# Local attention and a tanh-shrink feed-forward on one core: FP32 loads of the second tile's q and k, two fused distance operations, slope matrices made by two engines

## The chip, the cores and the metric

The program runs on one NeuronCore of a Trainium2 chip. A core has five engines, each with its own in-order instruction stream: TensorE (PE, matmuls and transposes), VectorE (DVE), ScalarE (ACT), GpSimd (POOL) and SyncE (SP). Sixteen DMA engines move data between HBM and the on-chip memory (SBUF). A transfer is issued by SP, ACT or POOL. In the profile, the transfers that SP issues lie on queue q1, those of ACT on q10 and those of POOL on q0 ("software_dynamic"). Only the transfers on POOL's queue convert FP32 to BF16 on the way in this kernel.

The metric is the device time of one execution in microseconds (us). It is given as the median of several executions. The profile is of one further execution.

## The reference

The inputs q, k and v have the shape batch 4, heads 8, sequence 768, head size 64. The weights are 512 x 2048 and 2048 x 512. All are FP32.

```python
rel = pos[:, None] - pos[None, :]
is_global = pos[None, :] < 8
is_local = (rel >= 0) & (rel < 96)
keep = is_global | is_local
dist = where(is_global & ~is_local, 96, abs(rel))
slopes = 2.0 ** (-8.0 * (arange(8) + 1) / 8)
scores = where(keep, q @ k.T / 8 - slopes * dist, -1e9)
a = softmax(scores)
x = (a @ v)  as [3072, 512]            # tokens by heads*head size
h = x @ w_in                           # [3072, 2048]
out = (h - tanh(h)) @ w_out            # [3072, 512]
```

A query thus sees at most 96 keys before it (itself among them) and the first 8 keys of its sequence. For a tile of 128 queries this takes two tiles of keys, its own and the one before.

## The kernel before

**Tiles and steps.** The 3072 tokens are 24 tiles of 128 tokens, six for each batch. For each tile `u` the kernel loads k, q and v, transposes k and q (`T1`, `T`; `a_T`, on PE for the first eight tiles, lines 234 and 238; by DMA afterwards, line 242), and copies the transposes from PSUM to SBUF (`Te`, line 253). It then computes scores against the tile's own keys and those of the tile before (`S`, line 271), exponentiates them on ScalarE (`E`, line 279), multiplies with v (`AV`, lines 295 and 299), normalises (`R`, lines 307 and 308), and transposes the result (`X`, `Xe`, lines 322 and 331). The feed-forward follows in two matmul steps: `m1` (line 356, weights `w_in_bf`), a tanh on ScalarE and a subtraction on VectorE (lines 367 and 373), and `m2` (line 388, weights `w_out_bf`). Each weight matrix is loaded in eight pieces, named `i` (w_in) and `o` (w_out) here. One `m1` step of the first tiles needs two pieces of w_in.

**Mask and bias.** The distance term and the mask are one matrix product: `dT` holds the distances (2^20 where a key is not to be seen), `slopes` holds for each head an identity matrix times the head's negative slope. `bias` (line 128) multiplies the two. For the first three tiles this product is put into the PSUM bank before the scores are added (`B`). For the later tiles its exponential `mk` is multiplied in (lines 140 and 282). `dT` comes from an iota on GpSimd (line 100) and seven VectorE instructions (lines 106 to 118). `slopes` is eight VectorE instructions on the identity matrix `ident` (line 123), which GpSimd makes.

**Loads.** All loads but two are issued by GpSimd in one order, given by the string `LOADS` (line 408): `t` is a tile's k, q and v, `i` and `o` are weight pieces. They convert to BF16 on the way. The two exceptions are k and q of tile 0: SP and ScalarE load them as FP32 at the very start (`load_plain`, line 193), and ScalarE and VectorE convert them (`cast`, line 218).

**What sets the order.** Nothing is ordered at run time. A planner (`plan`, line 555) walks through a table of operations. Each has an engine, a planned duration, what it comes after, the buffers it takes and gives, and a priority. At each step the planner takes the operation that can start first by its own model. Operations made with `flex` may go to either of two engines. The instructions are issued to each engine in the planned order, so an engine whose next instruction waits holds up everything behind it. Gaps in PE's plan before 14 us are filled with matmuls on zeros (`warm`, line 348). Bias and scores hold one of two PSUM buffers named `big`; transposes, `m1` and `m2` share four named `one`. q and k before their transposition lie in five buffers `kq`.

Of the kernel before, what the change touches and what calls it, by code (L numbers as in the profile page):

```python
# [7 lines left out]

FP32 = mybir.dt.float32
BF16 = mybir.dt.bfloat16  # L10
AF = mybir.ActivationFunctionType
ALU = mybir.AluOpType
# [4 lines left out]
def kernel(  # L17
# [11 lines left out]
    nc = tc.nc  # L29

    B, H, S, Dh = q.shape
    P = 128
# [3 lines left out]
    G = int(n_global)  # L36
    L = int(n_local)
    scale = 1.0 / float(Dh) ** 0.5
    BIG = 2.0 ** 20

    DM = moe_w_in.shape[0]
    DFF = moe_w_in.shape[1]
# [4 lines left out]
    NV = 12  # L47
    KQ = 5
    ROWS = 4
    APART = 4  # L50
    BIASED = 3
    PE_T, PE_X = 8, 9
    HT = 3
    TJ = 4
# [9 lines left out]
        return (0, u, N0) if u < N0 else ((u - N0) // HT + 1, (u - N0) % HT, HT)  # L64

    cpool = ctx.enter_context(tc.tile_pool(name="const", bufs=1))
    stpool = ctx.enter_context(tc.tile_pool(name="stage", bufs=1))
    bpool = ctx.enter_context(tc.tile_pool(name="bpool", bufs=KQ))
    kpool = ctx.enter_context(tc.tile_pool(name="kpool", bufs=9))
    ppool = ctx.enter_context(tc.tile_pool(name="ppool", bufs=3))  # L70
# [9 lines left out]
    ident = cpool.tile([P, P], BF16, name="ident")  # L80
    mk = cpool.tile([P, H, 3, P], BF16, name="mk")
    dist = cpool.tile([P, 2, P], FP32, name="dist")
    tmp01 = cpool.tile([P, 2, 2, P], FP32, name="tmp01")
# [14 lines left out]
    def prepare():  # L98
        make_identity(nc, ident)
        nc.gpsimd.iota(  # L100
            dist, pattern=[[P, 2], [-1, P]], base=0, channel_multiplier=1,
            allow_small_or_imprecise_dtypes=True,
        )

    def dist_mask():
        nc.vector.tensor_scalar(
            out=tmp01[:, 0], in0=dist, scalar1=0.0, scalar2=BIG, op0=ALU.is_lt, op1=ALU.mult
        )
        nc.vector.tensor_scalar(
            out=tmp01[:, 1], in0=dist, scalar1=float(L), scalar2=BIG, op0=ALU.is_ge, op1=ALU.mult  # L110
        )
        nc.vector.tensor_tensor(out=tmp01[:, 0], in0=tmp01[:, 0], in1=tmp01[:, 1], op=ALU.max)
        nc.vector.tensor_tensor(out=dT[:, 1:3, :], in0=dist, in1=tmp01[:, 0], op=ALU.max)
        nc.vector.tensor_copy(out=dT[:, 0, :], in_=dT[:, 1, :])
        nc.vector.tensor_scalar(
            out=dT[:, 0, 0:G], in0=dT[:, 0, 0:G], scalar1=float(L), scalar2=None, op0=ALU.min
        )
        nc.vector.memset(dT[:, 2, 0:G], float(L))

    def build_slopes():  # L120
        for h in range(H):
            slope = 2.0 ** (-8.0 * (h + 1) / H)
            nc.vector.tensor_scalar(  # L123
                out=slopes[:, slot(h), :], in0=ident, scalar1=-slope / scale, scalar2=None, op0=ALU.mult
            )

    def bias(dst, m, a, stop):
# [20 lines left out]
    PE, ACT, DVE, POOL, SP = ENG.PE, ENG.Activation, ENG.DVE, ENG.Pool, ENG.SP  # L148
# [6 lines left out]
    def op(key, eng, us, fn, after=(), take=(), give=(), pri=0, dma=0.0, alt=None):  # L155
        ops[key] = dict(
            key=key, eng=eng, us=us, fn=fn, alt=alt, after=[a for a in after if a is not None],
            take=list(take), give=list(give), pri=pri, dma=dma,
        )

# [14 lines left out]
    kf, qf, vf = {}, {}, {}  # L175
    kq = {}
# [40 lines left out]
    def cast(u, j, src, eng):  # L217
        copy_on(eng)(out=kq_of(u)[:, j, :], in_=src.pop(u).rearrange("p a x -> p (a x)"))
# [186 lines left out]
    AHEAD = 5.0  # L405
    WARM = (1.3, 14.0)
    T_ROWS, T_LD, T_W, T_ST, T_DT, T_DX = 0.66, 0.95, 1.29, 0.7, 1.75, 0.9
    LOADS = "tttiiitiiitoooiotoiooot"
    first, n_of = [], {"t": 0, "i": 0, "o": 0}
    for c in LOADS + "t" * NU:  # L410
        if n_of[c] < (NU if c == "t" else WJ):
# [3 lines left out]
    prev = None  # L415
# [6 lines left out]
    for it in first:  # L422
        if it[0] != "t":
            load(it, 0.75, lambda it=it: load_w(it), T_W)
            continue
        u = it[1]
        for nm in ("vf", "kf", "qf") if u == 0 else ("kf", "qf", "vf"):
            key = ("ld", nm, u)
            if u == 0 and nm != "vf":
                op(key, SP, 0.6 if nm == "kf" else 0.0, lambda: None, dma=T_ROWS)  # L430
                continue
            after = []
            if nm == "vf" and u >= NV:
                after += [("AV", u - NV + 1), ("V", (u - NV) // NQ * NQ + NQ - 2)]
            rows = u < ROWS and nm != "vf"
            load(key, 0.7 if rows else 0.88, lambda u=u, nm=nm: load_bf(u, nm), T_ROWS if rows else T_LD,
                 after=after, take=["kq"] if nm == "kf" else [])
        if u == 0:
            op(("prep",), POOL, 0.7, prepare, after=[("issue", prev)])
            prev = ("prep",)  # L440

    op(("dT",), DVE, 2.0, dist_mask, after=[("prep",)], pri=-2)
    op(("sl",), DVE, 0.9, build_slopes, after=[("prep",), ("issue", ("dT",))], pri=-2)

    def flex(key, us, fn, **kw):
        alt = [(e, t) for e, t in us]
        op(key, alt[0][0], alt[0][1], fn, alt=alt, **kw)
# [3 lines left out]
    for g, us in enumerate(groups):  # L451
        b, o, n, m = shape1(g)
# [3 lines left out]

    for m in range(3):
        for a in range(2):
            op(("mk", m, a), PE, 0.22, lambda m=m, a=a: a_mk(m, a), after=[("dT",), ("sl",), ("AV", 1)],
               take=["one"], pri=1)  # L460
            op(("mke", m, a), ACT, 0.52, lambda m=m, a=a: a_mke(m, a), after=[("mk", m, a)],
               give=["one"], pri=1)

    for u in range(NU):
        i = u % NQ
        rk, rq, rv = ("ld", "kf", u), ("ld", "qf", u), ("ld", "vf", u)
        if u == 0:
            op(("cq", u), ACT, 0.45, lambda u=u: cast(u, 0, qf, ACT), after=[rq], take=["kq"], pri=-1)
            op(("ck", u), DVE, 0.55, lambda u=u: cast(u, 1, kf, DVE), after=[rk, ("issue", ("cq", u))], pri=-1)
            rk, rq = ("ck", u), ("cq", u)  # L470
        go = [key for a, key in prog if a <= u - AHEAD]
        late = [("issue", ("T", u - 1)) if u else None, go[-1] if go else None]
# [16 lines left out]
        if u < BIASED:  # L489
            for o in os:  # L490
                op(("B", u, o), PE, 0.44, lambda u=u, o=o: a_B(u, o), pri=1,
                   after=[("dT",), ("sl",), ("issue", ("B", u, 0) if o else ("S", u - 1, 0)) if u or o else None],
                   take=["big"])
# [41 lines left out]
    for u in range(NU):  # L535
        g = group_of[u]
        m = shape1(g)[3]
# [17 lines left out]
    def plan():  # L555
# [2 lines left out]
        avail = {n: [0.0] * c for n, c in bufs.items()}  # L558
        free = {PE: WARM[0], ACT: 2.8, DVE: 1.5, POOL: 0.85, SP: 0.7}
        avail["one"][0] = WARM[1]  # L560
        ring = {SP: [0.0, []], POOL: [0.0, []]}
        share = {SP: 0.35, POOL: 0.65}
        done, start = {}, {}
        f1 = f2 = 0.0
# [9 lines left out]
        while waiting or any(queues.values()):  # L574
# [46 lines left out]
            end = t + o["us"]  # L621
            free[o["eng"]] = end
            start[key] = t
            if o["dma"]:
# [39 lines left out]
        return sorted(order, key=lambda x: x[0])  # L664

    with tc.manual_schedule(engines={PE, ACT, DVE, POOL, SP}):
        load_plain(0, "kf")
        load_plain(0, "qf")
        for i in range(2):
            nc.vector.memset(vb[i][:, :, Dh : Dh + 1], 1.0)  # L670
        nc.vector.memset(zero, 0.0)
        for i in range(2, NV):
            nc.vector.memset(vb[i][:, :, Dh : Dh + 1], 1.0)
        for t, key in with_warm(order):
            ops[key]["fn"]()
# [35 lines left out]
```

## Time and profile before

| what | value |
|---|---|
| median of 6 executions | 221.61 us (218.98 to 222.41) |
| profiled execution, its time | 221.1 us |
| its span, first to last instruction | 219.3 us |
| PE busy | 207.9 us (95%) |
| DVE, ACT, POOL busy | 132.7, 124.8, 73.1 us |
| warming matmuls within PE's busy time (line 348) | 4.9 us |
| granted TensorE clock | 1.0 in every stretch asked for |
| DMA queue of POOL (q0) | 13.37 MB |
| DMA queues of SP (q1) and ACT (q10) | 12.72 and 0.26 MB |

Times within the profile count from the start of the span. "Busy" is the time in which an engine executes. Matmuls are pipelined, so PE's busy time is not PE at its peak. The bytes of a queue are counted as they are written: a converting load reads twice what it is credited with. The profile's DMA share is the mean busy share of the sixteen DMA engines; it can be over 1[...]. A "landing" is the time from the start of a transfer's issue to its completion.

### The profile page before, as it was taken

How to read it: one execution, taken by the hardware profiler on the slowest of the kernel's cores; microseconds unless marked ns; L12 is line 12 of the kernel's file. 1: busy time of each engine (PE TensorE's matmuls, PEld its weight loads, DVE VectorE, ACT ScalarE, POOL GpSimd, SP SyncE). 2: the span in 40 equal slices, each digit the busy share in tenths (PEclk: the TensorE clock that was granted, in tenths of full speed). 3: DMA queues.
4: the chain of work that ended last, by engine and by line, in shares of the span. 5: the costliest groups of instructions: out<-in, count | busy, mean ns of one | idle time of the engine just before them, and what ended most of it. 6: DMA issues, size and time to landing. Idle time of an engine off the chain costs nothing.

```text
span 219.3 us, 5048 instructions
## 1 busy us (share of the span) xinstructions
PE 207.9 (95%) x2019; PEld 127.7 (58%) x2048; DVE 132.7 (61%) x285; ACT 124.8 (57%) x206; POOL 73.1 (33%) x93
## 2 busy tenths in 40 slices
PE   7779999999999999899979999999999999999994
PEld 2545997787766555455545555555555555555553
DVE  5536887668758866467647566666874744444311
ACT  3448988666558556565654754686564455544310
POOL 7968668798354604441327040000000000000000
PEclk9999999999999999999999999999999999999999
DMA  8999999999999999999999999331342121011112
GB/s 134 135 171 187 186 186 197 170 182 149 122 176 156 181 131 184 201 157 114 140 176 117 151 67 148 99 108 40 96 113 36 45 72 49 6 46 48 48 51 96
DMA packets 103960, 26.68 MB, mean 122 GB/s; under 512 B 92416, under 2 KB 100992, under 8 KB 103936
## 3 DMA queue, kind: packets, MB, share of 16 engines
q0 software_dynamic: 74592, 13.37, 79.9%
q1 hardware_dynamic: 29072, 12.72, 29.2%
q10 hardware_dynamic: 272, 0.26, 0.5%
q8 instruction: 16, 0.26, 0.5%
q14 instruction: 8, 0.07, 0.1%
HBM read 27.26 MB, written 6.29 MB: 153 GB/s over the span
## 4 chain that ended last, share of the span: by engine, by line
PE 82%; DMA 11%; POOL 2%; DVE 2%; issue 1%; POOLq 0%
PE one L356 35%; PE one L388 34%; DMA qk<-kq 8%; PE big L271 5%; DMA kq<-in_k_dram 4%; PE big L295 2%; PE big L299 2%; POOL w_in_bf L212 1%; PE one L322 1%; PE one L234 1%; POOL vb L199 1%; PE one L238 1%; DVE slopes L123 1%; PE one L128 0%; PE big L128 0%
## 5 line engine op out<-in xcount | busy, mean ns | idle before, releaser
L356 PE MATMUL one<-xT,w_in_bf 128*128 128x128 bf16 (+1 forms) x768 | 98.8, 273 | 1.6 <-DMA w_in_bf<-in_moe_w_in_dram 1.6
L367 ACT ACTIVATE th<-one 128x384 f32<-128x384 f32 (+1 forms) x120 | 61.2, 516 | 58.2 <-PE one L356 56.7
L388 PE MATMUL one<-w_out_bf,g 128*128 128x512 bf16 (+2 forms) x390 | 92.3, 362 | 1.7 <-issue 0.6
L373 DVE TENSOR_TENSOR g<-one,th 128x384 bf16<-128x384 f32 (+1 forms) x120 | 68.5, 581 | 40.6 <-ACT th L367 39.2
L356 PEld LDWEIGHTS <-w_in_bf 128*128 128x128 bf16 x768 | 58.8, 98 | 33.8 <-DMA w_in_bf<-in_moe_w_in_dram 2.1
L388 PEld LDWEIGHTS <-g 128*128 128x128 bf16 x416 | 37.6, 98 | 32.8
L205 POOL DMA_DIRECT2D kq<-in_k_dram x20 | 17.7, 885 | 43.7 <-DMA qk<-kq 37.5
L279 ACT ACTIVATE pd<-big 128x1024 bf16<-128x1024 f32 x24 | 24.6, 1023 | 5.0 <-PE big L271 5.0
L199 POOL DMA_DIRECT2D vb<-in_v_dram x24 | 21.5, 896 | 5.5 <-DMA kq<-in_k_dram 3.5
L282 DVE TENSOR_TENSOR pd<-pd,mk 128x1024 bf16<-128x1024 bf16 x21 | 14.5, 690 | 11.4 <-ACT pd L279 11.4
L279 ACT ACTIVATE po<-big 128x1024 bf16<-128x1024 f32 x20 | 20.5, 1026 | 1.1 <-PE big L271 1.1
L398 ACT COPY ot<-one 128x512 f32<-128x512 f32 (+1 forms) x19 | 10.9, 575 | 13.3 <-PE one L388 12.3
L205 POOL DMA_DIRECT2D kq<-in_q_dram x20 | 17.8, 890 | 1.8 <-DMA vb<-in_v_dram 0.8
L308 DVE TENSOR_TENSOR x<-big,rden 128x512 bf16<-128x512 f32 x24 | 16.6, 692 | 0.8
L271 PE MATMUL big<-qk 64*128 64x128 bf16 x352 | 14.4, 218 | 2.1 <-DMA qk<-kq 2.1
L271 PEld LDWEIGHTS <-qk 64*128 64x128 bf16 x352 | 9.9, 94 | 8.9 <-issue 4.8
L282 DVE TENSOR_TENSOR po<-po,mk 128x1024 bf16<-128x1024 bf16 x18 | 12.4, 690 | 2.9 <-ACT po L279 2.9
L295 PE MATMUL big<-vb,pd 128*128 128x65 bf16 x192 | 14.0, 193 | 0.0
L295 PEld LDWEIGHTS <-pd 128*128 128x128 bf16 x192 | 12.5, 97 | 1.8
L299 PE MATMUL big<-vb,po 128*128 128x65 bf16 x160 | 12.4, 193 | 0.0
L299 PEld LDWEIGHTS <-po 128*128 128x128 bf16 x160 | 10.4, 97 | 1.3
L398 DVE COPY ot<-one 128x512 f32<-128x512 f32 (+1 forms) x7 | 4.0, 578 | 8.9 <-PE one L388 7.0
(45 smaller groups left out, 85.3 us busy)
## 6 DMA issues: line engine op xcount, KB each, us to landing
out_dram<-ot SPq DMA_DIRECT2D x23, 256.0 KB, 2.8
vb<-in_v_dram POOLq DMA_DIRECT2D x24, 128.0 KB, 7.6
kq<-in_k_dram POOLq DMA_DIRECT2D x23, 128.0 KB, 7.0
kq<-in_q_dram POOLq DMA_DIRECT2D x23, 128.0 KB, 7.6
w_in_bf<-in_moe_w_in_dram POOLq DMA_DIRECT2D x8, 256.0 KB, 8.6
w_out_bf<-in_moe_w_out_dram POOLq DMA_DIRECT2D x8, 256.0 KB, 8.7
qf<-in_q_dram ACTq DMA_DIRECT2D x1, 256.0 KB, 3.4
kf<-in_k_dram SPq DMA_DIRECT2D x1, 256.0 KB, 4.0
```

The costliest lines, as they stand in the source:

```text
L199: i = nc.gpsimd.dma_start(out=vb[u % NV][:, :, 0:Dh], in_=by_head)
L205: i = nc.gpsimd.dma_start(out=dst.rearrange("p (h d) -> p h d", d=Dh), in_=by_head)
L271: nc.tensor.matmul(s[:, slot(2 * p + hh), :], qk[u - o][r, 1, p, :], qk[u][r, 0, p, :], start=u >= BIASED, stop=True, skip_group_check=u < ...
L279: nc.scalar.activation(pr[u, o], s, AF.Exp, bias=0.0, scale=scale)
L282: nc.vector.tensor_tensor(out=pr[u, o], in0=pr[u, o], in1=mk[:, :, mask_of(u, o), :], op=ALU.mult)
L295: nc.tensor.matmul(dst, pr[u, 0][:, slot(h), :], vb[u % NV][:, h, :], start=True, stop=last,)
L299: nc.tensor.matmul(dst, pr[u, 1][:, slot(h), :], vb[(u - 1) % NV][:, h, :], start=False, stop=True,)
L308: nc.vector.tensor_tensor(out=xs[u].rearrange("q (a h) d -> q a h d", a=2), in0=t[:, :, :, 0:Dh], in1=rden.to_broadcast([P, 2, H // 2, Dh] ...
L356: nc.tensor.matmul(t[:, (f - f0) * n : (f - f0 + 1) * n], w_in_bf[j][:, c, fo : fo + P], xT[b][:, c, o : o + n], start=(c == 0), stop=(c = ...
L367: nc.scalar.activation(h_view(ths[g, f0], g), h_view(hs[g, f0], g), AF.Tanh, bias=0.0, scale=1.0)
L373: nc.vector.tensor_tensor(out=gs[b][:, f0 : f0 + m, o : o + n], in0=h_view(hs.pop((g, f0)), g), in1=h_view(ths.pop((g, f0)), g), op=ALU.su ...
L388: nc.tensor.matmul(os_[u, part][:, 0 : hi - lo], gs[b][:, f, t * P : (t + 1) * P], w_out_bf[f // FJ][:, f % FJ, lo:hi], start=(f == 0), st ...
```

## The change

- **Loads.** k and q of tile 1 are loaded like those of tile 0: FP32, k by SP and q by ScalarE, issued directly behind those of tile 0 at the start, then converted on ScalarE or VectorE as the planner chooses (`PLAIN = 2`, two staging buffers each). The two converting loads of GpSimd go away. In `LOADS`, the fourth piece of w_in moves ahead of tile 3's k, q and v.
- **Planner.** The plan takes the four FP32 loads as landed at given times, 4.1 and 4.8 us (q and k of tile 0) and 1.4 us later for tile 1. GpSimd's transfers are modelled as starting to move at 5.2 us. The conversions of both tiles go to either engine (`flex`).
- **Distances.** Of the seven VectorE instructions, the copy, the cap and the memset stay. The two comparisons and the two maxima over 128 x 256 elements become four `scalar_tensor_tensor` instructions over 128 x 128, two for each half (`distance_0`, `distance_1`). For this GpSimd makes a second iota, `over`. The bias of a tile's own keys waits for the first half only.
- **Slopes.** Each of the eight is an operation of its own; VectorE makes two and ScalarE six, by an activation with a scale.
- **Start.** VectorE fills the identity's zeros instead of GpSimd; GpSimd, instead of VectorE, sets the ones column of the first v buffer.

```diff
-    LOADS = "tttiiitiiitoooiotoiooot"
+    LOADS = "tttiiiitiitoooiotoiooot"
...
-            if u == 0 and nm != "vf":
-                op(key, SP, 0.6 if nm == "kf" else 0.0, lambda: None, dma=T_ROWS)
+            if u < PLAIN and nm != "vf":
+                op(key, SP, 0.0, lambda: None, at=(4.8 if nm == "kf" else 4.1) + 1.4 * u, pri=-3,
+                   take=["kq"] if nm == "kf" else [])
                 continue
...
+    def unit():
+        nc.gpsimd.affine_select(
+            out=ident, in_=ident, compare_op=ALU.not_equal, fill=1.0, base=0,
+            pattern=[[-1, P]], channel_multiplier=1,
+        )
+
+    def numbers():
+        for t, base in ((dist, 0), (over, 1 - L)):
+            nc.gpsimd.iota(
+                t, pattern=[[P, 2], [-1, P]], base=base, channel_multiplier=1,
+                allow_small_or_imprecise_dtypes=True,
+            )
+
+    def distance(a):
+        n = slice(a, a + 1)
+        nc.vector.scalar_tensor_tensor(
+            out=dist[:, n], in0=dist[:, n], scalar=-FAR, in1=dist[:, n], op0=ALU.mult, op1=ALU.max
+        )
+        nc.vector.scalar_tensor_tensor(
+            out=dT[:, 1 + a, :], in0=over[:, a], scalar=FAR, in1=dist[:, a], op0=ALU.mult, op1=ALU.max
+        )
...
+    def slope(h, eng):
+        f = -(2.0 ** (-8.0 * (h + 1) / H)) / scale
+        if eng is ACT:
+            nc.scalar.activation(slopes[:, slot(h), :], ident, AF.Copy, bias=0.0, scale=f)
+        else:
             nc.vector.tensor_scalar(
-                out=slopes[:, slot(h), :], in0=ident, scalar1=-slope / scale, scalar2=None, op0=ALU.mult
+                out=slopes[:, slot(h), :], in0=ident, scalar1=f, scalar2=None, op0=ALU.mult
             )
...
-    op(("dT",), DVE, 2.0, dist_mask, after=[("prep",)], pri=-2)
-    op(("sl",), DVE, 0.9, build_slopes, after=[("prep",), ("issue", ("dT",))], pri=-2)
+            op(("ident",), POOL, 0.3, unit, after=[("issue", prev)])
+            op(("nums",), POOL, 0.7, numbers, after=[("issue", ("ident",))])
+            prev = ("nums",)
+
+    op(("dT", 0), DVE, 1.0, distance_0, after=[("nums",)], pri=-2)
+    op(("dT", 1), DVE, 0.6, distance_1, after=[("nums",), ("issue", ("dT", 0))], pri=-1)
+    for h in range(H):
+        eng = DVE if h < 2 else ACT
+        op(("sl", h), eng, 0.14 if h < 2 else 0.22, lambda h=h, eng=eng: slope(h, eng), after=[("ident",)], pri=-3)
...
-        if u == 0:
-            op(("cq", u), ACT, 0.45, lambda u=u: cast(u, 0, qf, ACT), after=[rq], take=["kq"], pri=-1)
-            op(("ck", u), DVE, 0.55, lambda u=u: cast(u, 1, kf, DVE), after=[rk, ("issue", ("cq", u))], pri=-1)
+        if u < PLAIN:
+            flex(("cq", u), [(ACT, 0.55), (DVE, 0.6)], lambda eng, u=u: cast(u, 0, qf, eng), after=[rq], pri=-1)
+            flex(("ck", u), [(DVE, 0.6), (ACT, 0.55)], lambda eng, u=u: cast(u, 1, kf, eng), after=[rk], pri=-1)
...
-        ring = {SP: [0.0, []], POOL: [0.0, []]}
+        ring = {SP: [0.0, []], POOL: [5.2, []]}
...
-        load_plain(0, "kf")
-        load_plain(0, "qf")
-        for i in range(2):
-            nc.vector.memset(vb[i][:, :, Dh : Dh + 1], 1.0)
+        nc.gpsimd.memset(vb[0][:, :, Dh : Dh + 1], 1.0)
+        for u in range(PLAIN):
+            load_plain(u, "kf")
+            load_plain(u, "qf")
+        nc.vector.memset(ident, 0.0)
         nc.vector.memset(zero, 0.0)
-        for i in range(2, NV):
+        for i in range(1, NV):
             nc.vector.memset(vb[i][:, :, Dh : Dh + 1], 1.0)
```

More of the change, by code (lines that the diff above doesn't have):

```diff
@@ L6 @@
 from concourse._compat import with_exitstack
-from concourse.masks import make_identity
 FP32 = mybir.dt.float32
@@ L38 @@
     scale = 1.0 / float(Dh) ** 0.5
-    BIG = 2.0 ** 20
+    FAR = 2.0 ** 20
     DM = moe_w_in.shape[0]
@@ L51 @@
     BIASED = 3
+    PLAIN = 2
     PE_T, PE_X = 8, 9
@@ L66 @@
     cpool = ctx.enter_context(tc.tile_pool(name="const", bufs=1))
-    stpool = ctx.enter_context(tc.tile_pool(name="stage", bufs=1))
+    stpool = ctx.enter_context(tc.tile_pool(name="stage", bufs=PLAIN))
     bpool = ctx.enter_context(tc.tile_pool(name="bpool", bufs=KQ))
@@ L82 @@
     dist = cpool.tile([P, 2, P], FP32, name="dist")
-    tmp01 = cpool.tile([P, 2, 2, P], FP32, name="tmp01")
+    over = cpool.tile([P, 2, P], FP32, name="over")
     dT = cpool.tile([P, 3, P], BF16, name="dT")
@@ L95, in slot, with distance_0 @@
         return (h % 2) * NP + h // 2
[L98 to L102, printed above, removed]
-        )
-    def dist_mask():
-        nc.vector.tensor_scalar(
-            out=tmp01[:, 0], in0=dist, scalar1=0.0, scalar2=BIG, op0=ALU.is_lt, op1=ALU.mult
-        )
-        nc.vector.tensor_scalar(
-            out=tmp01[:, 1], in0=dist, scalar1=float(L), scalar2=BIG, op0=ALU.is_ge, op1=ALU.mult
-        )
-        nc.vector.tensor_tensor(out=tmp01[:, 0], in0=tmp01[:, 0], in1=tmp01[:, 1], op=ALU.max)
-        nc.vector.tensor_tensor(out=dT[:, 1:3, :], in0=dist, in1=tmp01[:, 0], op=ALU.max)
+    def unit():
+        nc.gpsimd.affine_select(
+            out=ident, in_=ident, compare_op=ALU.not_equal, fill=1.0, base=0,
+            pattern=[[-1, P]], channel_multiplier=1,
+        )
+    def numbers():
[8 more added lines that the diff above has]
+            out=dist[:, n], in0=dist[:, n], scalar=-FAR, in1=dist[:, n], op0=ALU.mult, op1=ALU.max
+        )
+        nc.vector.scalar_tensor_tensor(
+            out=dT[:, 1 + a, :], in0=over[:, a], scalar=FAR, in1=dist[:, a], op0=ALU.mult, op1=ALU.max
+        )
+    def distance_0():
+        distance(0)
         nc.vector.tensor_copy(out=dT[:, 0, :], in_=dT[:, 1, :])
@@ L117, in dist_mask, with distance_1 @@
         )
+    def distance_1():
+        distance(1)
         nc.vector.memset(dT[:, 2, 0:G], float(L))
-    def build_slopes():
-        for h in range(H):
-            slope = 2.0 ** (-8.0 * (h + 1) / H)
+    def slope(h, eng):
[3 more added lines that the diff above has]
+        else:
             nc.vector.tensor_scalar(
-                out=slopes[:, slot(h), :], in0=ident, scalar1=-slope / scale, scalar2=None, op0=ALU.mult
+                out=slopes[:, slot(h), :], in0=ident, scalar1=f, scalar2=None, op0=ALU.mult
             )
@@ L153, in copy_on, with op @@
         return {ACT: nc.scalar.copy, DVE: nc.vector.tensor_copy, POOL: nc.gpsimd.tensor_copy}[eng]
-    def op(key, eng, us, fn, after=(), take=(), give=(), pri=0, dma=0.0, alt=None):
+    def op(key, eng, us, fn, after=(), take=(), give=(), pri=0, dma=0.0, alt=None, at=None):
         ops[key] = dict(
-            key=key, eng=eng, us=us, fn=fn, alt=alt, after=[a for a in after if a is not None],
+            key=key, at=at, eng=eng, us=us, fn=fn, alt=alt, after=[a for a in after if a is not None],
             take=list(take), give=list(give), pri=pri, dma=dma,
@@ L438 @@
         if u == 0:
-            op(("prep",), POOL, 0.7, prepare, after=[("issue", prev)])
-            prev = ("prep",)
-    op(("dT",), DVE, 2.0, dist_mask, after=[("prep",)], pri=-2)
-    op(("sl",), DVE, 0.9, build_slopes, after=[("prep",), ("issue", ("dT",))], pri=-2)
+            op(("ident",), POOL, 0.3, unit, after=[("issue", prev)])
[6 more added lines that the diff above has]
+        op(("sl", h), eng, 0.14 if h < 2 else 0.22, lambda h=h, eng=eng: slope(h, eng), after=[("ident",)], pri=-3)
+    biased_by = [("dT", 0)] + [("sl", h) for h in range(H)]
     def flex(key, us, fn, **kw):
@@ L458 @@
         for a in range(2):
-            op(("mk", m, a), PE, 0.22, lambda m=m, a=a: a_mk(m, a), after=[("dT",), ("sl",), ("AV", 1)],
+            op(("mk", m, a), PE, 0.22, lambda m=m, a=a: a_mk(m, a), after=biased_by + [("dT", 1), ("AV", 1)],
                take=["one"], pri=1)
@@ L491 @@
                 op(("B", u, o), PE, 0.44, lambda u=u, o=o: a_B(u, o), pri=1,
-                   after=[("dT",), ("sl",), ("issue", ("B", u, 0) if o else ("S", u - 1, 0)) if u or o else None],
+                   after=biased_by + [("dT", 1) if o else None,
+                                    ("issue", ("B", u, 0) if o else ("S", u - 1, 0)) if u or o else None],
                    take=["big"])
@@ L623, in plan @@
             start[key] = t
-            if o["dma"]:
+            if o["at"]:
+                done[key] = o["at"]
+            elif o["dma"]:
                 via = POOL if o["eng"] is POOL else SP
```

## The prediction

> **What bounds the kernel now.** I read the page's engine rows first, then PE's busy time by stretches, then the time line and the chain of the first 20 us, then the DMA views.
>
> PE is busy 95% of the span, so the end is PE's work plus the time PE loses. The busy time by stretches, PE alone, says where it loses time (columns: stretch, its length, busy time, instructions, clock, DMA share, GB/s):
>
> ```profile
> 0.00:2.00 2.00, 0.75 (x2) 1.00 0.00 0
> 2.00:4.00 2.00, 2.00 (x6) 1.00 0.80 223
> 4.00:6.00 2.00, 1.56 (x4) 1.00 1.81 190
> 14.00:16.00 2.00, 0.65 (x9) 1.00 1.39 190
> 20.00:22.00 2.00, 2.00 (x31) 1.00 1.62 187
> 22.00:80.00 58.00, 57.26 (x814) 1.00 1.92 170
> 80.00:120.00 40.00, 37.68 (x316) 1.00 1.61 152
> ```
>
> From 22 to 80 us PE loses 0.7 us. From 0 to 22 us its busy times sum to 17.6 us, but 4.9 of these are the matmuls on zeros (line 348), so the useful work is 12.7 and the loss 9.3 us. The change touches only this start, and can win only some of the 9.3. The time line shows what they are:
>
> ```profile
> 1.24 1.00 POOL L199 DMA_DIRECT2D vb<-in_v_dram  x1 [0.80 <-DVE vb L673]
> 3.17 0.29 DVE L106 TENSOR_SCALAR tmp<-dist 128x256 f32<-128x256 f32 x1 [1.61 <-POOL dist L100]
> 4.51 0.89 POOL L199 DMA_DIRECT2D vb<-in_v_dram  x1
> 4.85 0.57 DVE L114 COPY dT<-dT 128x128 bf16<-128x128 bf16 x1
> 5.65 1.15 DVE L123 TENSOR_SCALAR slopes<-ident 128x128 bf16<-128x128 bf16 x7
> 6.48 0.59 DVE L218 CAST kq<-kf 128x512 bf16<-128x512 f32 x1
> 6.50 0.72 PE L128 MATMUL big<-slopes,dT 128*128 128x512 bf16 x2 [0.94 <-DVE slopes L123]
> 7.16 2.03 PE L238 MATMUL one<-ident,kq 128*64 128x128 bf16 x32
> 14.60 0.62 PE L356 MATMUL one<-xT,w_in_bf 128*128 128x128 bf16 x8 [0.88 <-DMA w_in_bf<-in_moe_w_in_dram]
> 15.97 0.62 PE L356 MATMUL one<-xT,w_in_bf 128*128 128x128 bf16 x8 [0.75 <-DMA w_in_bf<-in_moe_w_in_dram]
> 18.00 0.63 PE L238 MATMUL one<-ident,kq 128*64 128x128 bf16 x8 [0.27 <-DMA kq<-in_k_dram]
> ```
>
> PE's first useful work is at 6.50, behind VectorE's distances and slopes. The conversion of k0 waits behind them too: k0 landed at 4.74 (issue at 0.74, 4.0 to landing), but the conversion starts at 6.48 and PE transposes at 7.16. Later PE waits 0.88, 0.75 and 0.27 us for weights and for k of tile 3, 1.9 in sum. While it waits, the work behind waits too, since PE's order is fixed.
>
> Asked one issue at a time, the DMA view gives the landings on POOL's queue (start of issue + time to landing): v0 5.7, k1 6.3, q1 7.0, v1 9.2, k2 9.9, q2 10.6, v2 13.2, w_in pieces 14.6, 15.9, 17.2, k3 18.0, q3 18.6, v3 19.6. The seconds' stretches show how full the DMA is (the last column is GB/s as written):
>
> ```profile
> 3.00:4.00 1.00, 1.00 (x4) 0.39 (x3) 0.79 (x3) 0.00 (x0) 1.00 (x3) 1.00 1.05 362
> 6.00:7.00 1.00, 0.49 (x2) 0.10 (x1) 1.00 (x8) 0.00 (x0) 1.00 (x3) 1.00 1.18 124
> 7.00:8.00 1.00, 1.00 (x17) 0.84 (x18) 0.06 (x1) 0.17 (x1) 1.00 (x2) 1.00 1.51 109
> ```
>
> Before 2 us nothing moves; from 3 to 4 us the FP32 loads of tile 0 run alone at 362 GB/s; near 7 us the rate dips (73 GB/s in the quarter 6.50 to 6.75), because v1, issued from 4.51 to 5.40, is not yet flowing and k1 and q1 are through.
>
> **The parts, costed.** The sum is against the profiled execution, 221.1 us with a span of 219.3; the 1.8 us around the span I leave as they are. The median, 221.6, is 0.5 above it; my forecast for the median is 221.6 minus the gain.
>
> *POOL's stream.* Two issues go (line 203, 0.71 us each: -1.42). The fill of the identity goes to VectorE (-0.23), a second iota comes (+0.35). The v0 issue now waits for POOL's own small memset (four like it take 0.10 each), not for VectorE: it starts at about 0.9 instead of 1.24 (bounds 0.8 and 1.24). So v1, k2, q2, v2 and the weights are issued 1.42 + 0.23 + 0.3 - 0.35 = 1.6 us earlier.
>
> *The transfers.* k1 and q1 took 0.55 and 0.7 us between landings on POOL's queue, 1.25 together. As FP32 they write 0.52 MB; at 362 GB/s that is 1.45 us, but on the same engines. Here the Trainium skill speaks against the change: "DMA: Bandwidth & Descriptors", section "Rules for kernel authors", says that spreading loads over several issuing engines gives no bandwidth, only issue time. By that rule the weights gain nothing (+0.2 by the numbers). By the rows they gain the dip at 6.5 to 7.4 us, when the engines have little to move since POOL has not issued yet: about half of 0.9 us, and part of the second wide gap (v2's 2.6 us against 1.0 for v3, with issues far ahead). Bounds for the second piece of w_in, which `m1` needs: from +0.2 to -(1.2 + 1.6 + 0.6) = -3.4, if v1 and v2 also fall to 1.0. The nearest rows are v1's and v2's own, so I keep their durations and take -0.6 + 0.2, rounded to -0.5: 15.4 us.
>
> *When FP32 q1 and k1 land.* They queue behind tile 0's on SP and ACT. At 3.7 us some 0.32 MB of 1.05 have moved (the quarter-second rates before, added up), and v0 starts to flow. The other 0.73 MB take 1.95 us alone, and v0, then v1 cost 0.9 us each: 6.5 with v0's part alone, 7.5 with both. I take 7.0, converted at 7.6.
>
> *VectorE.* From about 2.95 (POOL's iotas) it runs four fused operations. No such row exists; the nearest are a two-input operation over 256 elements, 0.42, and a one-input one over 128, 0.16, so 0.28 each, bounds 0.16 and 0.42. With the copy (0.16 to 0.57: the 0.57 ended with POOL's v1 issue at 5.40), the cap (0.17) and the memset (0.07), all is done at 4.5 to 5.2. The conversion of k0 then starts on landing, 4.75 to 5.2, instead of 6.48.
>
> *ScalarE.* A second DMA issue (0.71) goes ahead of the table load, which ends at 3.5 instead of 2.76. Six slopes follow: lines 279 and 367 give 1.02 us for 1024 and 0.60 for 512 elements, so 0.27 for 128; bounds 0.16 and 0.37 (the copy of 256). They end at 5.1. Queued behind them is q0's conversion, 5.1 to 5.7 instead of 4.13 to 4.75; its reader on PE comes after k0's transposes, so the cost hides. The last slope releases the first bias at 5.1 instead of 6.50.
>
> *PE.* Bias at 5.1, transposes of k0 at 5.4, of q0 at 5.9, then a wait until 7.6 for tile 1 with about 0.8 us of bias and scores to fill it. Work begins 1.4 us earlier, of which 0.3 are lost waiting: 1.1 won. With the bias earlier, tile 0's exponential starts near 7.9 instead of 9.56, and PE has more attention to do before it reaches `m1`.
>
> *Order of loads.* k3 comes behind a fourth piece of w_in: one 1.3 us step later, 18.8 after the other gains. Two pieces let PE do `m1` for three tiles, 0.9 us each: 2.7 us, which covers the 0.8. Without that cover it costs 0.8.
>
> Sum: 1.1 from the start and 0.5 from the weights: **1.6 us**, 219.5 for a profiled execution, **220.0** as a median. After 22 us PE stays the bound, so the shift carries to the end.
>
> **Rivals.**
>
> *Large gain (218.6).* With a deeper backlog v1 and v2 take about 1.7 us each instead of 2.2 and 2.6; the weights come 1.4 us earlier still, which takes away the rest of PE's waits for weights (0.88 + 0.75, of which 0.5 are counted): 1.6 + 1.4 = 3.0 us, if attention fills PE until then. For it: v3 took 1.0. Against: v2 had its issue ahead and still took 2.6.
>
> *No gain (221.6).* The rule holds: the engines are full, k1 and q1 land at 7.6, which with conversion is 8.2, when PE transposed tile 1 before (the second half of the 32 from 7.16). What VectorE wins is spent on warming matmuls. Or the new order of the whole plan costs later what it wins: the stretch from 80 to 120 us loses 2.3 us to single waits for transposing DMAs, and these may move either way.
>
> *Slower (223.8).* One mechanism: PE stands at tile 1's transposes. In the old order all 32 transposes run ahead of the first scores. If FP32 and converting loads share the engines by turns from 3.7 us on, the FP32 loads get two thirds of the mixed 160 to 187 GB/s (5 to 6 us), some 115: 0.73 MB take 6.3 us and land at 10.0. Conversion and transposes then come at 10.6 instead of 8.2, 2.4 us late, less 0.2 for weights. It decides from a landing of 7.6 on and costs over 1% from about 9.8. Against: at 4.00 to 4.25 both flowed and 305 GB/s were moved. For: the plan assumes 5.5 and 6.2, so all is ordered for an early landing.
>
> That the change does nothing it says is not open: the issues are fixed in the program.
>
> **How the numbers follow.** Within 1% (2.2 us) a measurement of this kernel hardly tells a change; six runs spread over 3.4 us. The likeliest case (gain 0.8 to 2.8) has 0.46: 0.19 of it below 219.4, 0.27 within 1%. Large gain 0.19, faster. No gain 0.15, within. Slower 0.20: 0.18 beyond 1%, 0.02 within. In sum 0.38, 0.44, 0.18. The likeliest case alone spans 218.8 to 220.8. The range for 8 in 10 goes from 217.9 (the large gain and 0.7 for the runs' spread) to 223.2 (most of the slower case).
>
> **What the profile after would show.** Bias matmuls near 5.1 and transposes near 5.4; q1 and k1 landed by 7.0, no PE wait over 1 us at tile 1's transposes; POOL's v1 issue near 2.9; the second w_in piece at 15.4 or before; PE full from about 20 us. Wrong would be: a landing of k1 after 9 us, exponentials of tile 0 not before 9, or a loss after 22 us that is more than 1.5 us off the 7.0 of before (0.7 to 80 us, 2.3 to 120 us, 4.0 for the rest and the last stores).

## The result, and the profile after

The changed kernel takes 0.9944 of the time before, with a 95% interval of 0.9925 to 0.9963. On the 221.09 us before (median of 64 executions) this is a gain of 1.2 us (0.8 to 1.7). The median after is 219.73 us (29 executions). All ratios leave out executions that took over 1.5% longer than the fastest of their kernel, here five of the 29. The profiled executions differ by 1.8 us: 219.3 against 221.1, with spans of 217.5 and 219.3. The forecast was 1.6 us. The sum came out near, but two of its terms did not: the first scores came 0.3 us earlier where 1.1 were forecast, and the weights 2.5 us earlier instead of 0.5.

PE's busy time by stretches, PE alone, with the columns as in the prediction. First a row of the kernel before, then the changed kernel:

```profile
0.00:14.00 14.00, 11.37 (x102) 1.00 1.15 139
```

```profile
0.00:14.00 14.00, 10.71 (x111) 1.00 1.28 182
...
14.00:16.00 2.00, 1.95 (x35) 1.00 1.45 195
...
22.00:80.00 58.00, 57.26 (x790) 1.00 1.92 168
80.00:120.00 40.00, 37.41 (x316) 1.00 1.57 154
```

The busy times from 0 to 22 us sum to 18.2 us, of which 3.5 are matmuls on zeros. The loss is 7.3 us instead of 9.3. Without the matmuls on zeros (4.9 and 3.5 us, all before 14 us) PE has done 7.2 us of work by 14 us instead of 6.5. From 14 to 22 us it does 7.5 instead of 6.2, most of it from 14 to 16 us, where it is busy for 1.95 us instead of 0.65. From 22 to 80 us nothing changes. From 80 to 120 us PE loses 0.3 us more. This makes 1.7 of the 1.8 us of the span.

The first scores and the first exponential of the kernel before:

```profile
9.12 0.40 PE L271 MATMUL big<-qk 64*128 64x128 bf16 x8
...
9.56 1.02 ACT L279 ACTIVATE pd<-big 128x1024 bf16<-128x1024 f32 x1 [0.21 <-PE big L271]
```

The time line of the changed kernel:

```profile
3.29 0.89 POOL L212 DMA_DIRECT2D vb<-in_v_dram  x1
...
4.59 0.95 PE L141 MATMUL big<-slopes,dT 128*128 128x512 bf16 x2 [0.58 <-DVE dist L113]
...
4.98 0.43 DVE L231 CAST kq<-kf 128x512 bf16<-128x512 f32 x1
...
5.65 0.62 ACT L231 CAST kq<-qf 128x512 bf16<-128x512 f32 x1 [0.41 <-DMA qf<-in_q_dram]
...
7.51 0.69 DVE L231 CAST kq<-kf 128x512 bf16<-128x512 f32 x1 [2.11 <-DMA kf<-in_k_dram]
...
8.25 0.63 PE L251 MATMUL one<-ident,kq 128*64 128x128 bf16 x8 [1.15 <-DVE kq L231]
...
8.82 0.40 PE L284 MATMUL big<-qk 64*128 64x128 bf16 x8
...
9.26 1.02 ACT L292 ACTIVATE pd<-big 128x1024 bf16<-128x1024 f32 x1 [1.83 <-PE big L284]
...
13.81 1.07 PE L369 MATMUL one<-xT,w_in_bf 128*128 128x128 bf16 x16
```

The bias is out at 4.59 us instead of 6.50, and k0 is converted at 4.98 instead of 6.48. But k1 lands only at 7.5 us. Its transposes stand ahead of the first scores in PE's order, so PE waits 1.15 us and the scores start at 8.82. That is 0.3 us earlier than before. The last line is the other half: both `m1` steps run in one go at 13.81, with no wait for weights.

The landings on GpSimd's queue, taken from the DMA view one issue at a time:

| | v1 issued | v0 lands | v1 takes | v2 takes | second w_in piece lands |
|---|---|---|---|---|---|
| before | 4.5 | 5.7 | 2.2 | 2.6 | 15.9 |
| after | 3.3 | 7.8 | 0.9 | 0.9 | 13.4 |

"Takes" is the time since the landing ahead of it in the queue. v0 lands 2.1 us later than before, since it shares the DMA engines with the FP32 loads. v1 and v2 behind it then take less than half the time.

What the queue moved from the landing ahead of v1 to that of the second w_in piece stands in the next two rows (packets, MB, mean busy share of the sixteen engines), first for the kernel before (6.99 to 15.92 us), then for the changed one (7.75 to 13.42 us):

```profile
q0 software_dynamic: 4112, 1.35, 137.9%
```

```profile
q0 software_dynamic: 2983, 1.07, 160.4%
```

This makes 151 GB/s before and 189 after. From share, length and number follows the mean time of a packet, 48 ns before and 49 after. So the packets did not take longer before; fewer were under way at a time. The queue is practically alone here, so a share over 1 means that the times of packets of one queue overlap within an engine. The second difference is in the bytes. The transfers from v1 to the second w_in piece (four of 128 KB, two of 256 KB) hold 1.05 MB in both kernels. Before, 0.3 MB more had been moved when that piece was complete. This points to engines that were already at the transfers behind it while others still had part of it to do; the trace does not name the engine of a packet.

Stretches of 1 us (PE alone; the last column is GB/s as written) show the same. The first row is from the kernel before, the others from the changed one:

```profile
11.00:12.00 1.00, 1.00 (x17) 1.00 1.24 150
```

```profile
7.00:8.00 1.00, 0.10 (x1) 1.00 1.90 178
...
11.00:12.00 1.00, 0.93 (x18) 1.00 1.46 198
```

From 7 to 8 us the kernel before moved 109 GB/s at a share of 1.51.

### The profile page after: what moved, and what is told of

The parts are those of the page before. It is cut to its first block, busy times and chain, and to the rows that moved or that the text cites. A ratio compares the mean times of both kernels' runs of the same rounds, so it can differ in the third digit from the quotient of the medians.

```text
span 217.5 us, 5049 instructions
## 1 busy us (share of the span) xinstructions
PE 206.6 (95%) x2016; PEld 127.1 (58%) x2044; DVE 132.1 (61%) x278; ACT 127.3 (59%) x215; POOL 72.0 (33%) x92
## 4 chain that ended last, share of the span: by engine, by line
PE 81%; DMA 12%; POOL 4%; issue 1%; DVE 0%; POOLq 0%
PE one L369 35%; PE one L401 34%; DMA qk<-kq 8%; PE big L284 5%; DMA kq<-in_q_dram 4%; PE big L308 2%; PE big L312 2%; POOL w_in_bf L225 1%; POOL vb L212 1%; PE one L247 1%; POOL kq L216 1%; PE one L335 1%; PE one L141 0%; PE one L251 0%; POOL over L106 0%
## 5 line engine op out<-in xcount | busy, mean ns | idle before, releaser
L411 ACT COPY ot<-one 128x512 f32<-128x512 f32 (+1 forms) x19 | 10.9, 574 | 13.3 <-PE one L401 12.9
```

## The experiments

All ratios are against the kernel before, run on the same chip in the same session. The row of the changed kernel is the measurement above, so it is compared with the others across sessions. Every reading of a trace is of one profiled execution.

| kernel | executions counted | ratio | 95% interval |
|---|---|---|---|
| changed kernel | 24 of 29 | 0.9944 | 0.9925 to 0.9963 |
| undo_loads | 21 of 22 | 0.9962 | 0.9946 to 0.9979 |
| loads_alone | 18 of 22 | 0.9932 | 0.9909 to 0.9955 |
| undo_order | 15 of 16 | 0.9940 | 0.9919 to 0.9962 |
| pool_delay | 18 of 20 | 1.0039 | 1.0016 to 1.0063 |
| dummy_loads | 10 of 10 | 0.9970 | 0.9938 to 1.0003 |
| k1_true | 5 of 5 | 0.9892 | 0.9865 to 0.9919 |
| k1_true_again | 9 of 9 | 0.9907 | 0.9876 to 0.9938 |
| loads_alone_k1 | 10 of 10 | 0.9919 | 0.9884 to 0.9955 |
| scores_first | 6 of 6 | 0.9898 | 0.9853 to 0.9943 |
| v0_late | 3 of 6 | 0.9873 | 0.9813 to 0.9932 |
| v0_late_scores_first | 18 of 19 | 0.9915 | 0.9887 to 0.9942 |
| warm_fill | 6 of 6 | 0.9855 | 0.9802 to 0.9909 |

### Loads or vector work

`undo_loads` takes the FP32 loads of tile 1 back and keeps the rest:

```diff
-    PLAIN = 2
+    PLAIN = 1
...
-        ring = {SP: [0.0, []], POOL: [5.2, []]}
+        ring = {SP: [0.0, []], POOL: [0.0, []]}
```

> The changed kernel with k and q of tile 1 again as converting loads of GpSimd (and the plan's start of GpSimd's transfers back at 0); distances, slopes and the order of loads stay as changed. Theory 'loads': the gain comes from weights that land 2.5 us earlier because GpSimd's queue has two transfers fewer; then the second piece of w_in lands at 15 us or later, PE waits for it again (over 1 us in sum before 20 us), and the time is 220.6 to 221.3, like before. Rival 'vector work': the gain comes from bias and conversions that start 1.9 us earlier; then the time stays at 219.5 to 220.0.

The ratio is 0.9962 (220.1 us). The second w_in piece lands at 15.2, v1 and v2 take 1.9 and 2.0 us, and PE waits 0.8 us for weights (over 1 was expected) and 2.3 for k of later tiles. So the weights are back where the theory "loads" put them. The time lies between the two theories: 0.4% of gain stay (0.2 to 0.5).

`loads_alone` is the kernel before with the FP32 loads, their times in the plan, their conversions by either engine and the order of loads from the change. Distances and slopes stay as they were:

```diff
...
+            if u < PLAIN and nm != "vf":
+                op(key, SP, 0.0, lambda: None, at=(4.8 if nm == "kf" else 4.1) + 1.4 * u, pri=-3,
+                   take=["kq"] if nm == "kf" else [])
...
+        for u in range(PLAIN):
+            load_plain(u, "kf")
+            load_plain(u, "qf")
```

> The kernel before with only the loads changed: FP32 loads of tile 1, the plan's times for them and the fourth piece of w_in ahead of tile 3; distances and slopes as before, all on VectorE, identity and its zeros by GpSimd. Theory 'loads': 219.6 to 220.3, the second piece of w_in lands by 14 us, no wait of PE for weights. Rival 'vector work': 220.8 to 221.5, first scores not before 9 us.

The ratio is 0.9932. The second w_in piece lands at 13.3, v1 and v2 take 1.1 and 1.0 us, and PE does not wait for weights. The first exponential starts at 9.11, 0.15 us before that of the changed kernel, though the vector work is the old one. The loads alone therefore bring all of the gain that can be measured. The vector work, with the new order of loads, brings 0.4% alone and nothing measurable on top. The two do not add.

### Why the weights come earlier

`pool_delay` keeps the FP32 loads and puts five iotas that nobody needs behind GpSimd's own two. v1 is then issued at 5.5 instead of 3.3 us:

```diff
...
+        for _ in range(5):
+            nc.gpsimd.iota(
+                idle, pattern=[[P, 2], [-1, P]], base=0, channel_multiplier=1,
+                allow_small_or_imprecise_dtypes=True,
+            )
```

> The changed kernel with five more iotas on GpSimd (into a tile that nobody reads) behind its own two: 1.9 us, so that v1 is issued at about 5.2, as far ahead of its turn as in the kernel before; the FP32 loads stay. Theory 'lead': v1 and v2 took 2.2 and 2.6 us in the kernel before because their descriptors were written only just ahead; then v2 takes over 1.8 us between landings again, the second piece of w_in lands at 15 us or later and the time goes to 220.5 or more. Rival 'two transfers fewer': v1 and v2 keep their 0.9 us, the second piece lands by 14.2, the time within 0.6 of the changed kernel.

The ratio is 1.0039, so a delay of 2.2 us on GpSimd costs all of the gain and more. v1 takes 1.3 and v2 1.6 us (over 1.8 was expected), the two w_in pieces behind them 1.9 and 2.4 us. The second lands at 16.9, 3.5 us later than in the changed kernel, which is more than the delay itself. The first row is from this kernel, the second from the changed one:

```profile
14.00:15.00 1.00, 1.00 (x11) 1.00 1.38 159
```

```profile
14.00:15.00 1.00, 1.00 (x24) 1.00 1.44 195
```

`dummy_loads` goes the other way. It is the kernel before with two useless FP32 loads behind those of tile 0:

```diff
+        for nm, src, eng in (("kx", k, nc.sync), ("qx", q, nc.scalar)):
+            eng.dma_start(out=stpool.tile([P, 2, TJ * Dh], FP32, name=nm), in_=rows_of(src, 1))
```

> The kernel before with two useless loads added: k and q of tile 1 as FP32 by SP and ScalarE into tiles that nobody reads, behind those of tile 0; GpSimd still loads them converting, and all else is as before. 0.52 MB more are moved. Theory 'lead': the FP32 loads hold GpSimd's transfers back until about 7.5 us while their descriptors pile up; then v1 and v2 take 0.9 to 1.3 us between landings instead of 2.2 and 2.6, and the second piece of w_in lands at 14.6 to 15.9, no later than before in spite of the added bytes; time within 0.6 of before. Rival 'bytes': it lands 1.4 us later, 17.3, and the time rises by 1 us or more.

v0 lands at 8.1 us, then v1 and v2 take 1.0 us each, and the second w_in piece lands at 15.6. That is 0.3 us earlier than before, although 0.52 MB more were moved ahead of it and GpSimd issued it at the same time (8.44). The ratio is 0.9970, with an interval that just touches 1, although the first exponential starts at 10.92, 1.4 us later than before. From 14 us on the rate is that of the changed kernel:

```profile
14.00:15.00 1.00, 1.00 (x15) 1.00 1.45 197
```

Both runs agree with the lead and not with the number of bytes. The lead is here the time from the start of v1's issue to the landing ahead of it. It is 2.5 us in the kernel before, 2.6 in `undo_loads` and 2.1 in `pool_delay`, and there v1 takes 1.3 to 2.2 us. It is 3.9 to 5.4 us in the eleven others, and there v1 takes 0.9 to 1.2 us.

The lead of v1 is not the whole of it. v2 had a lead of 3.8 us in the kernel before and took 2.6 us; in `k1_true_again` it had the same and took 1.0. And a landing can be late with a long lead: in `k1_true` the fourth w_in piece was issued 5.6 us before the landing ahead of it and still landed 2.6 us behind it. Why fewer packets are under way after a short lead no run here shows.

### The order of loads

`undo_order` puts the fourth piece of w_in back behind tile 3:

```diff
-    LOADS = "tttiiiitiitoooiotoiooot"
+    LOADS = "tttiiitiiitoooiotoiooot"
```

> The changed kernel with the old order of loads (fourth piece of w_in behind tile 3's k, q, v). Theory 'loads': the first two pieces still land at 13.4, k3 at about 15.5, the fourth piece at about 19; PE has 2.7 us less feed-forward work to fill up with between 16 and 19 us but tile 3 earlier: within 0.4 us of the changed kernel, 219.5 to 220.1. Rival 'order': the swap itself is what wins, and the time goes back to 220.7 or more.

The ratio is 0.9940, as for the changed kernel. k3 lands at 15.1 and the fourth piece at 18.3. The swap is worth nothing that can be measured.

### PE's wait for k1

`k1_true` sets the plan's landing times to those of the trace:

```diff
-                op(key, SP, 0.0, lambda: None, at=(4.8 if nm == "kf" else 4.1) + 1.4 * u, pri=-3,
+                op(key, SP, 0.0, lambda: None, at={"kf": (4.8, 7.5), "qf": (4.2, 5.65)}[nm][u], pri=-3,
```

> The changed kernel with the plan's landing times of the four FP32 loads set to those of the trace (q 4.2 and 5.65, k 4.8 and 7.5 us instead of 4.1 and 5.5, 4.8 and 6.2), nothing else. The first scores then stand ahead of tile 1's transposes on PE. Theory 'late k1': they start near 7.5 instead of 8.8, the exponential near 8 instead of 9.26, and the time falls by 0.4 to 1.2 us, to 218.5 to 219.3. Rival 'transfers set it': PE is fed by the weights from 13.4 us on whatever stands ahead, and the time stays within 0.3 of 219.7.

The ratio is 0.9892 (218.76 us). The same kernel was run a second time:

> The kernel of k1_true once more (the plan's landing times set to those of the trace), for more executions: 218.5 to 219.0, ratio 0.987 to 0.992.

It gave 0.9907. The scores start ahead of tile 1's transposes, as expected, at 7.7 us in the first profile. In the second:

```profile
7.38 0.40 PE L284 MATMUL big<-qk 64*128 64x128 bf16 x8
...
8.25 1.10 PE L251 MATMUL one<-ident,kq 128*64 128x128 bf16 x16
```

But the plan's later orders changed too, so this alone does not say which step wins. The same times on top of `loads_alone` give `loads_alone_k1`:

> The kernel before with the loads changed as in loads_alone, and the plan's landing times set to those of the trace as in k1_true; distances and slopes as before, all on VectorE. Theory 'late k1 hides the vector work': with k1's wait out of the way, the later bias (6.5 instead of 4.6 us) delays the first scores to about 9 instead of 7.5, and the time is 0.4 to 1.2 above k1_true, 219.2 to 220.0. Rival 'vector work is worth nothing': within 0.3 of k1_true.

The median is 219.56 us against 219.37 for `k1_true_again` in the same session (0.9919 and 0.9907). The scores start at 8.70 there, 1.3 us later, and this costs nothing that can be measured: 0.3 us, give or take 1.0 (an estimate from the two intervals).

Two runs changed one step and left all else in the plan's order. `scores_first` issues the first scores ahead of tile 1's transposes (`ahead`, in the lines left out, moves one step of the order in front of another):

```diff
     order, model_end = plan()
...
+    ahead(("S", 0, 0), ("T1", 1))
```

> The changed kernel with its plan unchanged but for one step: the first scores (tile 0) are issued ahead of the transposes of tile 1's k. All later orders are those of the changed kernel. Theory 'late k1': PE's wait for k1 (1.2 us at 8.25) no longer holds the scores; they start at 7.5 instead of 8.8, the exponential of tile 0 at 8.0 instead of 9.26, PE's loss before 22 us falls from 7.3 to 6.3 to 6.9 us, and the time falls by 0.4 to 1.0, to 218.7 to 219.3. Rival 'tile 1 sets it': the chain through tile 1's exponentials starts at k1's landing in any case, time within 0.3 of the changed kernel.

The ratio is 0.9898, but the gain did not come in the expected way. The scores start at 9.02, not at 7.5. In this execution q1 lands at 7.4 instead of 5.65, and ScalarE's order has the conversion of q1 ahead of the copy that the scores need:

```profile
7.37 0.62 ACT L231 CAST kq<-qf 128x512 bf16<-128x512 f32 x1 [2.13 <-DMA qf<-in_q_dram]
7.90 1.06 ACT L266 COPY qk<-one 128x512 bf16<-128x512 bf16 x2
```

`v0_late` lets GpSimd make the identity and the iotas first and issue v0 behind them, at 1.9 us instead of 1.28 (2.4 was expected):

```diff
...
+    ahead(("nums",), ("ld", "vf", 0))
+    ahead(("ident",), ("nums",))
```

> The changed kernel with its plan unchanged but for one step: GpSimd makes the identity and the two iotas first and issues v of tile 0 behind them, at about 2.4 instead of 1.28 us. Theory 'sharing': the FP32 loads run alone for 0.9 us longer, so k1 lands at 6.0 to 6.4 instead of 7.5 and q1 at 5.3 to 5.6; conversion and transposes of tile 1 start at 7.0 instead of 8.25; time 218.6 to 219.3. The weights' landings stay (13.4 for the second piece, within 0.4). Rival 'the second load on SP is late by itself': k1 still lands after 7.2 and the time stays within 0.3 of the changed kernel.

k1 lands at 6.4 us, as expected from less sharing, and tile 1's transposes start at 7.13 instead of 8.25. The second w_in piece lands at 12.9 (13.0 or later was expected). The ratio is 0.9873, with a wide interval, from three executions. The other three had a mean clock of 0.991 or 0.992 and took 221.6 to 221.9 us.

`v0_late_scores_first` does both:

> Both steps: v of tile 0 issued behind the iotas, and the first scores ahead of tile 1's transposes. If both act on the same wait of PE for k1, the two gains do not add: within 0.3 us of the better of the two, 218.5 to 219.2. If the start of the exponentials counts by itself, 218.2 to 218.6.

The ratio is 0.9915. The gains do not add. The point values of all these kernels lie below the changed kernel's, by 0.2 to 0.7% of the time. Only `k1_true` has an interval clear of it, its second set overlaps, and its later orders are others too. So a cost of k1's wait by itself is suggested but not shown, and the runs do not rank the remedies.

### Filling the wait

`warm_fill` puts five more matmuls on zeros ahead of tile 1's transposes:

```diff
         for t, key in with_warm(order):
+            if key == ("T1", 1):
+                for _ in range(5):
+                    warm()
             ops[key]["fn"]()
```

> The changed kernel with five more matmuls on zeros put on PE ahead of tile 1's transposes, to fill PE's wait from 7.1 to 8.25 us; nothing else. Theory 'clock': in 6 of 29 executions of the changed kernel the granted clock averages 0.990 to 0.992 and they take 221.9 us instead of 219.3; an idle PE near 8 us is what lets the clock fall. Then such executions become rarer (at most 1 in 10), the median comes to 219.2 to 219.5, and the executions at full clock stay at 219.3. Rival 'the later stall': it is the wait at 111 us (1.56) that lets the clock fall; then the share stays near 1 in 5.

The ratio is 0.9855, below the changed kernel's interval, and the fastest of all: 217.84 us (216.63 to 219.81). None of its six executions had a lowered mean clock, against 6 of 29 of the changed kernel. With so few this decides nothing. And the clock is not the reason for the time: executions at full clock came to 217.8, not to the expected 219.3. The matmuls even took longer than the wait, so the first scores start at 10.21, 1.4 us later. The profiled execution (218.8 us) is 0.5 us faster than that of the changed kernel, and its trace shows where these 0.5 us are won. PE by stretches from 80 to 120 us:

```profile
80.00:120.00 40.00, 39.31 (x342) 1.00 1.48 150
```

PE loses 0.7 us here instead of 2.6. In the changed kernel, the store of the output at 110.06 us is followed by the next at 119.53. With the fill they are at 110.95 and 118.80: 0.9 us later at first, 0.7 earlier afterwards. Between them lies PE's wait for a transposing load (1.56 us in the changed kernel, none over 0.4 with the fill). Five kernels have the changed kernel's later order and GpSimd on time. They reach the first of these stores at 109.90 (`v0_late_scores_first`), 109.98 (`v0_late`), 110.06, 110.50 (`scores_first`) and 110.95, and the second at 118.75, 119.68, 119.53, 119.31 and 118.80. The last at the first store is the second to reach the other. A lead or a lag at the start is thus partly lost or made up at this wait. That the later start itself shortens it is argued from one execution each and not shown, and why the median is lower still stays open.

## Why the prediction was right, and where its terms were not

- **What bounds the kernel.** Right: PE loses time up to 22 us, and little changes behind. The loss fell by 2.0 us, 0.3 went back between 80 and 120 us.
- **GpSimd's stream.** The step "it starts at about 0.9" was off: v0 is issued at 1.28, since GpSimd stands idle for 0.41 us behind its own memset. v1 is issued at 3.29, not 2.9, 1.2 us earlier than before instead of 1.6.
- **The transfers: the term that failed.** "The nearest rows are v1's and v2's own, so I keep their durations" gave 0.5 us. v1 and v2 took 0.9 us each, and the second w_in piece came 2.5 us earlier. The deeper backlog of the rival "large gain" was the right mechanism, and `pool_delay` and `dummy_loads` show it from both sides. Its sum was wrong all the same: the weights came earlier than its 1.9 us and both waits for weights are gone, but 1.2 us were won and not 3.0. Its condition, that attention fills PE until the weights come, was met only in part: by 14 us PE's work was only 0.7 us ahead. The objection to it, that v2 had its issue ahead and still took 2.6, is not answered by the runs.
- **The Trainium skill's rule** ("DMA: Bandwidth & Descriptors", section "Rules for kernel authors", spreading over issuing engines gives no bandwidth, only issue time) was weighed as speaking against the change. What it states is not refuted: the FP32 loads and GpSimd's did share, and v0 landed 2.1 us later. But issue time was not a small matter: with the FP32 loads ahead and v1 issued 1.2 us earlier, the second w_in piece came 2.5 us earlier, and with v1 issued 2.2 us later again (`pool_delay`) it came 3.5 us later.
- **When k1 lands.** 7.0 was forecast (6.5 to 7.5), 7.5 measured; q1 was early, at 5.65. The slower rival's mechanism was real, and the landing came within 0.1 us of the point from which it decides, with a PE wait of 1.15 us at its place. (0.73 MB at 362 GB/s take 2.0 us, not 1.95; this changes nothing.)
- **VectorE and ScalarE.** Four fused operations took 0.29 us each (0.28 forecast), six slopes 1.30 us (1.6), the bias came at 4.59 (5.1). The durations were right.
- **PE's start: the other term that failed.** 1.1 us were forecast, on "a wait until 7.6 for tile 1 with about 0.8 us of bias and scores to fill it". The first scores could not fill it: they stand behind tile 1's transposes in PE's order. So the scores came 0.3 us earlier and the exponential at 9.26, not 7.9. An exponential "not before 9" was one of the prediction's own signs of being wrong. What an earlier start would be worth stays open. In `undo_loads` an exponential 1.2 us earlier than before, at 8.38, goes with a gain of 0.8 us (0.5 to 1.2), of which weights that land 0.7 us earlier may be a part. In `loads_alone_k1` scores 1.3 us later cost nothing measurable.
- **Order of loads.** k3 landed at 16.8, not 18.8, and the swap cost nothing measurable, as costed.

In sum 1.1 + 0.5 = 1.6 us were forecast. In the profiled executions PE's work was 0.7 us ahead by 14 us, gained 1.3 more up to 22 us, where its waits of 0.88 and 0.75 us for weights are gone, and lost 0.3 again between 80 and 120 us: 1.7 of the 1.8 measured. How much of the 0.7 is the earlier start, and how much the earlier transfers of tiles 1 and 2, the stretches do not tell. That the total was right owes much to luck: one term was too large and the other too small.

## What to carry to other kernels

Before you cost a transfer by its own row, look at how far its issue ran ahead of the landing before it. Here the queue moved 151 GB/s with a short lead and 189 with a longer one, and the weights came 2.5 us earlier. A busy share over 1 is no sign of a full rate: it was 1.38 and 1.60. And an earlier start need not be worth its length: ask which wait ends last behind it. Matmuls that fill a wait are cheap to try, though how they won here is not shown.

## What the runs showed of the hardware

The granted TensorE clock fell to half in or shortly after short pauses of PE. In the profiled execution of `scores_first` PE paused for 1.6 us up to 9.02. PE in stretches of 1 us (the column behind the count is the clock):

```profile
8.00:9.00 1.00, 0.00 (x0) 1.00 1.72 178
9.00:10.00 1.00, 0.98 (x17) 1.00 1.99 173
10.00:11.00 1.00, 1.00 (x15) 0.57 1.49 193
...
13.00:14.00 1.00, 1.00 (x17) 0.72 1.45 195
```

The clock is at half for about 3.4 us (0.43, 0.5, 0.5 and 0.28 us lost in the four stretches from 10 us on, doubled), and it falls when PE is already at work again. The profiled execution of `loads_alone` shows the same far into the kernel, in a wait of 2.58 us for a transposing load that ends at 112.39:

```profile
111.00:112.00 1.00, 0.00 (x0) 0.98 1.61 103
...
113.00:114.00 1.00, 1.00 (x10) 0.50 0.91 203
...
115.00:116.00 1.00, 1.00 (x6) 0.82 1.69 108
```

The Trainium skill ("TensorE: Matmul & The Clock Gate", section "Part 1: The HAM clock gate (the "warmup" mystery)") names a free-running window of about 3.4 us for this, which agrees with the length. The times agree too: in `pool_delay` the clock averages 0.74 from 10 to 11 us and 0.65 from 116 to 117 us, so it falls at 10.48 and 116.30, 31 times 3.41 us apart. The section's table asks for an idle window of about 3.4 us before the clock falls; here a pause of 1.6 us was enough. Pauses of 1.2 us (the changed kernel) and 1.6 us (its wait at 111 us) did not lower it in the profiled execution. What decides is not shown. 3.4 us at half the clock are 1.7 us of PE's work, more than this change wins.

Executions with a lowered clock are not equally frequent. A mean clock of 0.992 or less was granted in 14 of 22 executions of `loads_alone`, against 3 of 53 of the kernel before in the same session. In the changed kernel it was 6 of 29, which took 221.9 us (median) where the others took 219.3.

The landing of the FP32 loads varied by 1.9 us between executions with the same instructions at the start: q1 lands at 5.65 us in the changed kernel, at 5.4 to 5.9 in five other profiled executions with this start, and at 7.4 in `scores_first`. A plan with fixed landing times cannot be right for all of them.
